# A deeper attention tail, norms two tiles ahead, padded denominators and warm-up matmuls in a four-layer kernel on one core

## Chip, cores, metric

The kernel runs on one core of one Trainium2 chip. The metric is the device time of one execution in microseconds (us); lower is better. A single-core program has one time per run; its runs are compared by their median, and a difference is called faster or slower only beyond 2%, with a 95% interval. All runs quoted are undisturbed ("fast").

Engine names as in the profile: PE is TensorE (matmuls), PEld its weight loads, DVE is VectorE, ACT is ScalarE, POOL is GpSimd, SP issues the DMAs.

## The reference

Four layers, A B A B, on x of 2048 tokens by 1024 features in bf16. A is linear attention with 32 heads of 32, B a gated linear unit with 3584 hidden features. The code is abridged here.

```python
def _A_ref(x, wqkv, wo):                       # x is layer-normed before the call
    q, k, v = split_heads(x @ wqkv)            # cut: reshape and transpose
    phi = lambda t: jnp.where(t > 0, t + 1, jnp.exp(t)) + 1e-6
    pq, pk = phi(q), phi(k)
    kv  = jnp.einsum("bhsd,bhse->bhde", pk, v)         # "KVA" below
    z   = jnp.einsum("bhsd->bhd", pk)
    num = jnp.einsum("bhqd,bhde->bhqe", pq, kv)        # "ND" below, with den
    den = jnp.einsum("bhqd,bhd->bhq", pq, z)[..., None] + 1e-6
    return merge_heads(num / den) @ wo                 # "OT", "WO" below

x = x + _A_ref(_layernorm(x), A_wqkv, A_wo)
x = x + _B_ref(_layernorm(x), B_w_gate, B_w_up, B_w_down)   # ((x Wg) * (x Wu)) Wd
# ... and both once more
```

## The kernel before

The program is recorded as a list of operations, each with the tiles that it reads and writes. From these the recorder derives dependencies, by *granules*: 256 bytes per partition in SBUF, one bank in PSUM. A list scheduler with estimated durations then fixes the order on each engine, and waits are emitted for the dependencies that the order doesn't cover. Note what it does for two operations on the same engine: TensorE is exempt from waiting on itself, the other engines are not.

```python
SB_GRAN = 256
...
        for d in sorted(op.deps, key=lambda o: -o.end):
            if d.eng == "pe" and e == "pe" and not d.dma_bytes:
                continue                       # no wait of PE on PE; DVE on DVE does wait
            if base.get(d.semkey, 0) >= d.sig:
                continue
            w.append((d.semkey, d.sig))
```

A layer A has three stages on TensorE. For each of 16 tiles of 128 tokens: the K and V projections (KVP, 32 matmuls of 512 columns) and the accumulation KVA (8 small matmuls). Then the Q projections (QP, 32 groups of 8). Then the *tail*: per tile ND (8 matmuls, numerator and denominator), a division on VectorE, OT (8 transposes), an eviction of OT from PSUM by ScalarE ("otev"), WO (16 matmuls of 512 columns), and the residual on VectorE. Layer norms run alongside, each ending in 8 transposes on TensorE (LT) and a copy on VectorE. In the first layer the norm of tile i is recorded just before the projections of tile i.

```python
    DEN = [view("DEN", r * SB_GRAN, H, F32) for r in range(2)]     # 32 floats, one granule
    RDEN = [view("RDEN", r * SB_GRAN, H, F32) for r in range(2)]
...
            if i + 1 < NT:                       # end of layer_A: the tail
                tail_pre(i + 1, par, kvb, 5)     # ND, division, OT, otev of the next tile
            tail_post(i, par, tb, [3, 4, 6])     # WO, residual, next norm of this tile
...
    def tail_pre(i, par, kvb, otbank):           # ND cut
            for k in range(nbk):                 # three PSUM banks
                dd = dn[:, 12 * k: 12 * k + 4 * n].rearrange(...)
                P.add("dve", ... eh.tensor_scalar(dd, src[:, :, 128:132], 1e-6, None, ALU.add), ...)
            P.add("dve", lambda eh, dn=dn, rd=rd: eh.reciprocal(rd, dn), ins=[dn], outs=[rd], ...)
            for (k, n, src) in srcs:             # o = numerator * reciprocal
                P.add("dve", ... eh.tensor_tensor(o4, n4, rb, ALU.mult), ...)
            P.add("pe", em_ot, ins=[ob, IDENT], outs=[pb[:, 0:NG * 128]], ...)
            P.add("act", ... eh.activation(otb, src, ACTF.Copy), ...)
```

## Time and profile before

| | before |
|---|---|
| median of 5 runs | 1714.61 us (1714.49 to 1714.73) |
| span of the profiled run | 1712.9 us |
| TensorE busy | 1687.5 us, 99% |
| late starts of TensorE, start and KV of layer one | 10.9 us |
| late starts of TensorE, both tails | 12.7 us |
| late starts elsewhere | under 0.5 us a stage |

"Late starts" needs a word. Matmuls are pipelined and their ends are modelled, so a TensorE that is "99% busy" may still lose time. But their starts come at a steady pace: 0.216 us for 512 columns, 0.056 to 0.059 us for 128 to 132. I took, from the trace, the gap between each matmul's start and the next one's, less the median gap for its source line, and summed by stage. That is the time that a change of order can win; the gated unit's stages have none.

From the page of the kernel before (busy table, then shares of the chain that ended last):

```profile
span 1712.9 us, 19994 instructions
...
PE 1687.5 (99%) x8704; PEld 799.2 (47%) x8704; DVE 749.0 (44%) x1227; ACT 356.3 (21%) x577; POOL 138.4 (8%) x261
...
PE 93%; ACT 3%; POOL 2%; issue 1%; DVE 0%; DMA 0%; POOLq 0%
```

The waits of TensorE in the kernel before (line that waited, who released it: us in total, times, longest):

```profile
PE ps L501 <- POOL arena L495: 8.8, 2, 8.6
PE ps L694 <- ACT arena L680: 7.9, 30, 0.7
PE ps L556 <- ACT arena L595: 2.9, 12, 0.2
```

L501 is LT, the first one behind the first norm. L694 is WO, waiting for the eviction of OT. L556 is KVA, waiting for the last V eviction.

The timeline of TensorE in the kernel before, at the start, in the KV stage of layer one and in the first tail (start us, duration us, engine, line, operation, count; in brackets the idle time before and what ended it):

```profile
8.65 1.04 PE L501 MATMUL ps<-arena 128*128 128x128 bf16 x8 [8.65 <-POOL arena L495]
10.47 6.38 PE L586 MATMUL ps<-arena 128*128 128x512 bf16 x16 [0.79 <-DVE arena L506]
...
62.15 0.64 PE L556 MATMUL ps<-arena 128*128 128x129 bf16 x8 [0.24 <-ACT arena L595]
...
70.46 0.63 PE L556 MATMUL ps<-arena 128*128 128x129 bf16 x8 [0.24 <-ACT arena L595]
...
223.13 3.63 PE L694 MATMUL ps<-arena 128*128 128x512 bf16 x16 [0.20 <-ACT arena L680]
226.59 0.61 PE L675 MATMUL ps<-arena 128*128 128x128 bf16 x8
227.04 0.61 PE L501 MATMUL ps<-arena 128*128 128x128 bf16 x8
227.49 0.63 PE L648 MATMUL ps<-arena 128*128 128x132 bf16 x8
228.32 1.04 PE L694 MATMUL ps<-arena 128*128 128x512 bf16 x4 [0.20 <-ACT arena L680]
```

Three readings. The first 16 KV matmuls take 6.38 us where 16 x 0.216 = 3.45 would do. A KV tile takes 70.46 - 62.15 = 8.31 us. A tail tile takes 228.32 - 223.13 = 5.19 us, of which the matmul starts fill 3.45 + 0.45 + 0.45 + 0.46 = 4.81; the rest stands before WO.

VectorE in the same tail tile of the kernel before (copy of LT, den, reciprocal, o, residual):

```profile
222.50 0.69 DVE L506 COPY arena<-ps 128x1024 bf16<-128x1024 bf16 x1 [0.19 <-PE ps L501]
223.11 0.56 DVE L661 TENSOR_SCALAR arena<-ps 128x12 f32<-128x12 f32 x3
223.71 0.35 DVE L663 RECIPROCAL arena<-arena 128x32 f32<-128x32 f32 x1
224.09 1.35 DVE L668 TENSOR_TENSOR arena<-ps,arena 128x384 bf16<-128x384 f32 x3
225.36 0.68 DVE L699 SCALAR_TENSOR_TENSOR arena<-ps,arena 128x512 f32<-128x512 f32 x1
```

The three den instructions of 0.16 to 0.17 us take 0.60 us until the reciprocal starts, so they don't overlap.

### The profile page before, as it was taken

To read this page: it belongs to the slowest core of one execution; us is meant where nothing else is said; L and a number is where in the kernel's file an instruction comes from. 1 tells how busy PE (TensorE), PEld (TensorE's weight loads), DVE (VectorE), ACT (ScalarE), POOL (GpSimd) and SP (SyncE) were. 2 spreads that over 40 slices of the span, in tenths; PEclk is the share of its full clock that TensorE was granted. 3 is DMA by queue.
4 is the path that set the end of the run, shared out by engine and by line. 5 is a ranking of instruction groups with operands and counts; after the bars stand their busy time and mean duration, and the time that the engine had idled before them with its cause. 6 is when DMAs were issued, how large, how long until landed. Compare 5 with 4: busy or idle time off the path is not lost.

```text
span 1712.9 us, 19994 instructions
## 1 busy us (share of the span) xinstructions
PE 1687.5 (99%) x8704; PEld 799.2 (47%) x8704; DVE 749.0 (44%) x1227; ACT 356.3 (21%) x577; POOL 138.4 (8%) x261
## 2 busy tenths in 40 slices
PE   7999999999999999999999999999999999999998
PEld 3444455444444444444454445544444444444444
DVE  7335775252424333333452367733343434242515
ACT  6323343101010111111343333421101010101010
POOL 5110043000000000000340001420000000000000
PEclk9999999999999999999999999999999999999999
DMA  7100102011010101020120001021010101010002
GB/s 251 44 1 1 50 1 75 28 47 49 25 50 25 49 25 49 25 74 25 50 75 1 1 1 50 1 74 50 25 50 25 50 25 50 25 49 25 1 24 99
DMA packets 55832, 70.49 MB, mean 41 GB/s; under 512 B 1472, under 2 KB 42432, under 8 KB 55744
## 3 DMA queue, kind: packets, MB, share of 16 engines
q1 hardware_dynamic: 55744, 69.21, 12.4%
q8 instruction: 68, 1.11, 0.3%
q14 instruction: 20, 0.16, 0.0%
HBM read 65.01 MB, written 4.19 MB: 40 GB/s over the span
## 4 chain that ended last, share of the span: by engine, by line
PE 93%; ACT 3%; POOL 2%; issue 1%; DVE 0%; DMA 0%; POOLq 0%
PE ps L730 45%; PE ps L753 21%; PE ps L586 12%; PE ps L694 7%; PE ps L624 6%; ACT arena L680 2%; POOL arena L495 1%; PE ps L556 1%; PE ps L675 1%; ACT arena L488 1%; POOL arena L492 1%; ACT arena L595 0%; PE ps L501 0%; POOL arena L490 0%; POOL arena L483 0%
## 5 line engine op out<-in xcount | busy, mean ns | idle before, releaser
L730 PE MATMUL ps<-arena 128*128 128x512 bf16 x3584 | 776.5, 379 | 0.0
L730 PEld LDWEIGHTS ps<-arena 128*128 128x128 bf16 x3584 | 350.4, 98 | 421.4
L739 DVE TENSOR_TENSOR arena<-ps,arena 128x512 bf16<-128x512 f32 x224 | 155.0, 692 | 601.5 <-PE ps L730 601.5
L753 PE MATMUL ps<-arena 128*128 128x512 bf16 x1792 | 390.9, 379 | 0.0
L737 ACT ACTIVATE arena<-ps 128x512 f32<-128x512 f32 x224 | 133.7, 597 | 964.0 <-PE ps L730 963.9
L759 DVE TENSOR_TENSOR arena<-ps,arena 128x1024 f32<-128x1024 f32 x192 | 235.2, 1225 | 102.8 <-PE ps L753 102.8
L753 PEld LDWEIGHTS ps<-arena 128*128 128x128 bf16 x1792 | 174.9, 98 | 208.8
L586 PE MATMUL ps<-arena 128*128 128x512 bf16 x1024 | 230.0, 382 | 0.8 <-DVE arena L506 0.8
L586 PEld LDWEIGHTS ps<-arena 128*128 128x128 bf16 x1024 | 98.6, 98 | 116.6 <-issue 3.6
L694 PE MATMUL ps<-arena 128*128 128x512 bf16 x512 | 116.1, 380 | 7.9 <-ACT arena L680 7.9
L512 DVE TENSOR_SCALAR arena<-arena 128x512 f32<-128x512 f32 x128 | 55.9, 436 | 145.7 <-ACT arena L511 145.7
L624 PE MATMUL ps<-arena 128*128 128x512 bf16 x512 | 111.5, 379 | 0.0
L511 ACT ACTIVATE arena<-ps 128x512 f32<-128x512 f32 x128 | 76.4, 597 | 165.3 <-PE ps L586 91.1
L514 DVE SCALAR_TENSOR_TENSOR arena<-ps,arena 128x512 bf16<-128x512 f32 x128 | 88.4, 691 | 3.9
L495 POOL TENSOR_SCALAR arena<-arena 128x1024 bf16<-128x1024 f32 x64 | 76.4, 1194 | 68.8 <-PE ps L501 63.7
L488 ACT ACTIVATE arena<-arena 128x1024 bf16<-128x1024 f32 x64 | 73.2, 1144 | 36.4 <-POOL arena L483 27.8
L694 PEld LDWEIGHTS ps<-arena 128*128 128x128 bf16 x512 | 47.6, 98 | 66.5 <-ACT arena L680 13.2
L624 PEld LDWEIGHTS ps<-arena 128*128 128x128 bf16 x512 | 49.9, 98 | 59.5
L506 DVE COPY arena<-ps 128x1024 bf16<-128x1024 bf16 x64 | 44.2, 690 | 41.3 <-PE ps L501 41.0
L699 DVE SCALAR_TENSOR_TENSOR arena<-ps,arena 128x512 f32<-128x512 f32 x64 | 44.0, 687 | 31.0 <-PE ps L694 31.0
L680 ACT ACTIVATE arena<-ps 128x1024 bf16<-128x1024 bf16 x32 | 32.8, 1024 | 92.9 <-PE ps L675 92.9
L483 POOL TENSOR_SCALAR arena<-arena 128x1 f32<-128x1 f32 x32 | 6.5, 202 | 560.2 <-DVE arena L763 550.2
(35 smaller groups left out, 434.2 us busy)
## 6 DMA issues: line engine op xcount, KB each, us to landing
arena<-in_B_w_gate_dram SPq DMA_DIRECT2D x14, 1024.0 KB, 5.4
arena<-in_B_w_up_dram SPq DMA_DIRECT2D x14, 1024.0 KB, 7.2
arena<-in_B_w_down_dram SPq DMA_DIRECT2D x14, 1024.0 KB, 5.5
arena<-in_A_x_dram SPq DMA_DIRECT2D x16, 256.0 KB, 3.3
arena<-in_A_wqkv_dram SPq DMA_DIRECT2D x8, 512.0 KB, 7.9
arena<-in_A_wqkv_dram SPq DMA_DIRECT2D x2, 2048.0 KB, 8.2
arena<-in_A_wo_dram SPq DMA_DIRECT2D x4, 1024.0 KB, 10.5
arena<-in_A_wqkv_dram SPq DMA_DIRECT2D x4, 1024.0 KB, 5.7
```

Of the source, the lines that this page charges most:

```text
L488: P.add("act", lambda eh: eh.activation(SQA, x, ACTF.Square, bias=st[:, 1:2], scale=1.0, accum_out=st[:, 2:3]), ins=[x, st[:, 1:2]], outs= ...
L495: P.add("pool", lambda eh: eh.tensor_scalar(lt, x, st[:, 1:2], st[:, 4:5], ALU.add, ALU.mult), ins=[x, st[:, 1:2], st[:, 4:5]], outs=[lt], ...
L511: P.add("act", lambda eh: eh.activation(et, pb_, ACTF.Exp), ins=[pb_], outs=[et], dur=act_t(fd), name="exp" + nm)
L514: P.add("dve", lambda eh: eh.scalar_tensor_tensor(dst, pb_, C1, et, ALU.add, ALU.max), ins=[pb_, et], outs=[(dst, dtag)], dur=dve_t(fd), n ...
L586: last = eh.matmul(pb_, LNT[:, dt_, i * 128:(i + 1) * 128], WKV[c][:, dt_, :], start=(dt_ == 0), stop=(dt_ == ND - 1))
L624: last = eh.matmul(pb_, WQ[:, dt_, g * 128:(g + 1) * 128], LNT[:, dt_, c * 512:(c + 1) * 512], start=(dt_ == 0), stop=(dt_ == ND - 1))
L694: last = eh.matmul(pb_, otb[:, g, :], WOW[cf][:, g, :], start=(g == 0), stop=(g == NG - 1))
L730: last = eh.matmul(pb_, W[:, dt_, jt * 128:(jt + 1) * 128], LNT[:, dt_, c * 512:(c + 1) * 512], start=(dt_ == 0), stop=(dt_ == ND - 1))
L737: P.add("act", lambda eh, gt=gt, pb_=pbs[0]: eh.activation(gt, pb_, ACTF.Copy), ins=[pbs[0]], outs=[gt], dur=act_t(512), name="gcp")
L739: P.add("dve", lambda eh, gt=gt, pb_=pbs[1], hd=hd: eh.tensor_tensor(hd, pb_, gt, ALU.mult), ins=[pbs[1], gt], outs=[(hd, "h%d" % jc)], du ...
L753: last = eh.matmul(pb_, HB[:, jt, i * 128:(i + 1) * 128], WD[:, jt, cf * FCW:(cf + 1) * FCW], start=(jt == 0), stop=(jt == 3))
L759: P.add("dve", lambda eh, i=i, acc=acc: eh.tensor_tensor(XRES[i], acc, XRES[i], ALU.add), ins=[acc, XRES[i]], outs=[XRES[i]], dur=dve_t(D) ...
```

## The change

The intent: keep TensorE from waiting. (1) 36 matmuls on a tile of ones while the first input is on its way, so that the clock is up when real work starts. (2) In the first layer, norms recorded two tiles ahead. (3) The tail split in two parts, with ND three tiles and OT two tiles ahead of WO. (4) den and rden slices 64 floats apart, so that each has a granule of its own, with one reciprocal per slice. Other buffers follow (three OT results; one set of statistics).

```diff
-HOIST = 2
+HOIST = 3
+NWARM = 36
...
-    alloc("O", 2 * D * 2); alloc("OTB", 2 * D * 2); ...
+    alloc("O", 2 * D * 2); alloc("OTB", 3 * D * 2); ...
-    DEN = [view("DEN", r * SB_GRAN, H, F32) for r in range(2)]
-    RDEN = [view("RDEN", r * SB_GRAN, H, F32) for r in range(2)]
+    DEN = [view("DEN", r * 3 * SB_GRAN, 192, F32) for r in range(2)]
+    RDEN = [view("RDEN", r * 3 * SB_GRAN, 192, F32) for r in range(2)]
...
+    def em_warm(eh):
+        for k in range(NWARM):
+            last = eh.matmul(bank(7, 256), onesb[:, 0:128], onesb[:, 0:256], start=True, stop=True)
+        return last
...
-                ln_chain(i, par, tb)
+                for ia in ([0, 1, 2] if i == 0 else [i + 2]):
+                    if ia < NT:
+                        first_ln(ia)
...
-                    tail_pre(0, par, kvb, tb)
+                    nd_part(0, par, kvb)
+                    ot_part(0, tb)
+                    if NT > 1:
+                        nd_part(1, par, kvb)
+                        ot_part(1, 5)
+                    if NT > 2:
+                        nd_part(2, par, kvb)
...
-            if i + 1 < NT:
-                tail_pre(i + 1, par, kvb, 5)
+            if i + 2 < NT:
+                ot_part(i + 2, 5)
+            if i + 3 < NT:
+                nd_part(i + 3, par, kvb)
             tail_post(i, par, tb, [3, 4, 6])
...
-            dd = dn[:, 12 * k: 12 * k + 4 * n]
+            dd = dn[:, 64 * k: 64 * k + 4 * n]
...
-        P.add("dve", lambda eh, dn=dn, rd=rd: eh.reciprocal(rd, dn), ins=[dn], outs=[rd], ...)
         for (k, n, src) in srcs:
+            P.add("dve", lambda eh, dk=dk, rk=rk: eh.reciprocal(rk, dk), ins=[dk], outs=[rk], ...)
```

More of the change, by code (lines that the diff above doesn't have):

```diff
@@ L387, in _build @@
     alloc("PK", NR * D * 2); alloc("VAUG", NR * NG * 132 * 2); alloc("ET", 4 * 512 * 4)
-    alloc("O", 2 * D * 2); alloc("OTB", 2 * D * 2); alloc("LNTOK", 2 * D * 2); lay["OUTS"] = lay["PK"]
+    alloc("O", 2 * D * 2); alloc("OTB", 3 * D * 2); alloc("LNTOK", 2 * D * 2); lay["OUTS"] = lay["PK"]
     alloc("KVZ", NG * 132 * 2); alloc("SQA", D * 2); lay["SQD"] = lay["O"]
-    alloc("DEN", 2 * SB_GRAN); alloc("RDEN", 2 * SB_GRAN); alloc("STAT", 2 * NT * SB_GRAN)
+    alloc("DEN", 2 * 3 * SB_GRAN); alloc("RDEN", 2 * 3 * SB_GRAN); alloc("STAT", NT * SB_GRAN)
     alloc("IDENT", 128 * 2); alloc("BMASK", 128 * 4); alloc("E4", 4 * 4); alloc("NEGH", 4); alloc("ONES", 128 * 4)
@@ L421, in _build @@
     XS = [view("O", r * D * 2, D, BF16) for r in range(4)]
-    OTB = [v3("OTB", r * D * 2, NG, 128, BF16) for r in range(2)]
+    OTB = [v3("OTB", r * D * 2, NG, 128, BF16) for r in range(3)]
     LNTOK = [view("LNTOK", r * D * 2, D, BF16) for r in range(2)]
@@ L427, in _build @@
     SQA = view("SQA", 0, D, BF16); SQD = view("SQD", 0, D, BF16)
-    DEN = [view("DEN", r * SB_GRAN, H, F32) for r in range(2)]
-    RDEN = [view("RDEN", r * SB_GRAN, H, F32) for r in range(2)]
-    STAT = [[view("STAT", (par * NT + i) * SB_GRAN, 8, F32) for i in range(NT)] for par in range(2)]
+    DEN = [view("DEN", r * 3 * SB_GRAN, 192, F32) for r in range(2)]
+    RDEN = [view("RDEN", r * 3 * SB_GRAN, 192, F32) for r in range(2)]
+    STAT = [[view("STAT", i * SB_GRAN, 8, F32) for i in range(NT)] for par in range(2)]
     IDENT = view("IDENT", 0, 128, BF16); BMASK = view("BMASK", 0, 128, F32)
@@ L470, in _build @@
           ins=[ONES], outs=[IDENT], dur=400, name="ident")
+    onesb = ONES.bitcast(BF16)
+    def em_warm(eh):
+        for k in range(NWARM):
+            last = eh.matmul(bank(7, 256), onesb[:, 0:128], onesb[:, 0:256], start=True, stop=True)
+        return last
+    if NWARM > 0:
+        P.add("pe", em_warm, ins=[ONES], outs=[bank(7, 256)], dur=NWARM * 150.0, name="warm")
     ctr = {"lntok": 0, "ring4": 0, "pair": 0, "pkv": 0, "et": 0, "o": 0, "otb": 0, "den": 0, "gu": 0, "dn": 0, "outs": 0, "wor": 0}
@@ L547, in late_loads, with first_ln @@
                 dma("sp", WOW[c][:], wo_src[:, :, c * FCW:(c + 1) * FCW], 128 * NG * FCW * 2, "ld_wo", tag="wo")
-        pend_kva = []
+        fl_state = {"rest": first_rest}
+        def first_ln(i):
+            if fl_state["rest"] is None:
+                late_loads()
+                fl_state["rest"] = []
+            for i2 in range(i, min(NT, i + 4)):
+                if i2 not in xslot:
+                    ldx(i2)
+                    fl_state["rest"].remove(i2)
+                    if not fl_state["rest"]:
+                        late_loads()
+            st = STAT[par][i]
+            P.add("dve", lambda eh, i=i, st=st, xs=xslot[i]: eh.tensor_scalar(XRES[i], xs, 1.0, None, ALU.mult, ALU.add, accum_out=st[:, 0:1]),
+                  ins=[xslot[i]], outs=[XRES[i], st[:, 0:1]], dur=dve_t(D), name="rowsum%d" % i)
+            if i == 0:
+                add_const1()
+            ln_chain(i, par, tb)
         def add_kva(i, r):
@@ L563, in layer_A @@
             if first:
-                if first_rest is None:
-                    late_loads()
-                    first_rest = []
-                for i2 in range(i, min(NT, i + 4)):
-                    if i2 not in xslot:
-                        ldx(i2)
-                        first_rest.remove(i2)
-                        if not first_rest:
-                            late_loads()
-                st = STAT[par][i]
-                P.add("dve", lambda eh, i=i, st=st, xs=xslot[i]: eh.tensor_scalar(XRES[i], xs, 1.0, None, ALU.mult, ALU.add, accum_out=st[:, 0:1]),
-                      ins=[xslot[i]], outs=[XRES[i], st[:, 0:1]], dur=dve_t(D), name="rowsum%d" % i)
-                if i == 0:
-                    add_const1()
-                ln_chain(i, par, tb)
+                for ia in ([0, 1, 2] if i == 0 else [i + 2]):
+                    if ia < NT:
+                        first_ln(ia)
             r = nxt("pkv", NR)
@@ L630, in layer_A @@
         if not hoisted:
-            tail_pre(0, par, kvb, 5)
+            nd_part(0, par, kvb)
+            ot_part(0, 5)
+            if NT > 1:
+                nd_part(1, par, kvb)
+                ot_part(1, 5)
+            if NT > 2:
+                nd_part(2, par, kvb)
         for i in range(NT):
-            if i + 1 < NT:
-                tail_pre(i + 1, par, kvb, 5)
+            if i + 2 < NT:
+                ot_part(i + 2, 5)
+            if i + 3 < NT:
+                nd_part(i + 3, par, kvb)
             tail_post(i, par, tb, [3, 4, 6])
@@ L638, in _build, with nd_part @@
     otbs = {}
-    def tail_pre(i, par, kvb, otbank):
+    obs = {}
+    def nd_part(i, par, kvb):
         nbk = (NG + 2) // 3
-        if True:
-            c, ii = i // 4, i % 4
-            def em_nd(eh, c=c, ii=ii):
-                for g in range(NG):
-                    lh = PQT[c][:, g, ii * 128:(ii + 1) * 128]
-                    last = eh.matmul(bank(kvb[g // 3], 132, (g % 3) * 132), lh, KVZ[:, g, 0:132], start=True, stop=True)
-                return last
-            P.add("pe", em_nd, ins=[(PQT[c][:, :, ii * 128:(ii + 1) * 128], "pqt"), KVZ[:]], outs=[bank(kvb[k]) for k in range(nbk)],
-                  dur=NG * 58.0, name="ND%d" % i)
-            r = nxt("den", 2)
-            dn, rd = DEN[r], RDEN[r]
-            ob = OB[nxt("o", 2)]
-            srcs = []
-            for k in range(nbk):
-                n = min(3, NG - 3 * k)
-                src = ps[:, kvb[k] * 512: kvb[k] * 512 + n * 132].rearrange("p (a b) -> p a b", a=n)
-                srcs.append((k, n, src))
-                dd = dn[:, 12 * k: 12 * k + 4 * n].rearrange("p (a b) -> p a b", a=n)
-                P.add("dve", lambda eh, dd=dd, src=src: eh.tensor_scalar(dd, src[:, :, 128:132], 1e-6, None, ALU.add),
-                      ins=[src[:, :, 128:132]], outs=[dn[:, 12 * k: 12 * k + 4 * n]], dur=120, name="den%d" % i)
-            P.add("dve", lambda eh, dn=dn, rd=rd: eh.reciprocal(rd, dn), ins=[dn], outs=[rd], dur=65 + 8 * H / 0.96, name="rden%d" % i)
-            for (k, n, src) in srcs:
-                o4 = ob[:, 384 * k: 384 * k + 128 * n].rearrange("p (a h e) -> p a h e", a=n, h=4)
-                n4 = src[:, :, 0:128].rearrange("p a (h e) -> p a h e", h=4)
-                rb = rd[:, 12 * k: 12 * k + 4 * n].rearrange("p (a h) -> p a h", a=n).unsqueeze(3).to_broadcast([128, n, 4, 32])
-                P.add("dve", lambda eh, o4=o4, n4=n4, rb=rb: eh.tensor_tensor(o4, n4, rb, ALU.mult),
-                      ins=[src[:, :, 0:128], rd[:, 12 * k: 12 * k + 4 * n]], outs=[ob[:, 384 * k: 384 * k + 128 * n]],
-                      dur=dve_t(128 * n), name="o%d" % i)
-            pb = bankb(otbank)
-            def em_ot(eh, ob=ob, pb=pb):
-                for g in range(NG):
-                    last = eh.transpose(pb[:, g * 128:(g + 1) * 128], ob[:, g * 128:(g + 1) * 128], IDENT)
-                return last
-            P.add("pe", em_ot, ins=[ob, IDENT], outs=[pb[:, 0:NG * 128]], dur=NG * 56.0, name="OT%d" % i)
-            otb = OTB[nxt("otb", 2)]
-            src = pb[:, 0:NG * 128].rearrange("p (a b) -> p a b", a=NG)
-            P.add("act", lambda eh, otb=otb, src=src: eh.activation(otb, src, ACTF.Copy), ins=[src], outs=[otb[:]],
-                  dur=act_t(NG * 128), name="otev%d" % i)
-            otbs[i] = otb
@@ new lines, in nd_part, with em_nd @@
+        c, ii = i // 4, i % 4
+        def em_nd(eh, c=c, ii=ii):
+            for g in range(NG):
+                lh = PQT[c][:, g, ii * 128:(ii + 1) * 128]
+                last = eh.matmul(bank(kvb[g // 3], 132, (g % 3) * 132), lh, KVZ[:, g, 0:132], start=True, stop=True)
+            return last
+        P.add("pe", em_nd, ins=[(PQT[c][:, :, ii * 128:(ii + 1) * 128], "pqt"), KVZ[:]], outs=[bank(kvb[k]) for k in range(nbk)],
+              dur=NG * 58.0, name="ND%d" % i)
+        r = nxt("den", 2)
@@ new lines, in nd_part @@
+        dn, rd = DEN[r], RDEN[r]
+        ob = OB[nxt("o", 2)]
+        obs[i] = ob
+        srcs = []
+        for k in range(nbk):
+            n = min(3, NG - 3 * k)
+            src = ps[:, kvb[k] * 512: kvb[k] * 512 + n * 132].rearrange("p (a b) -> p a b", a=n)
+            srcs.append((k, n, src))
+            dd = dn[:, 64 * k: 64 * k + 4 * n].rearrange("p (a b) -> p a b", a=n)
+            P.add("dve", lambda eh, dd=dd, src=src: eh.tensor_scalar(dd, src[:, :, 128:132], 1e-6, None, ALU.add),
+                  ins=[src[:, :, 128:132]], outs=[dn[:, 64 * k: 64 * k + 4 * n]], dur=120, name="den%d" % i)
@@ new lines, in nd_part @@
+        for (k, n, src) in srcs:
+            dk = dn[:, 64 * k: 64 * k + 4 * n]
+            rk = rd[:, 64 * k: 64 * k + 4 * n]
+            P.add("dve", lambda eh, dk=dk, rk=rk: eh.reciprocal(rk, dk), ins=[dk], outs=[rk], dur=65 + 8 * 4 * n / 0.96, name="rden%d" % i)
+            o4 = ob[:, 384 * k: 384 * k + 128 * n].rearrange("p (a h e) -> p a h e", a=n, h=4)
+            n4 = src[:, :, 0:128].rearrange("p a (h e) -> p a h e", h=4)
+            rb = rk.rearrange("p (a h) -> p a h", a=n).unsqueeze(3).to_broadcast([128, n, 4, 32])
+            P.add("dve", lambda eh, o4=o4, n4=n4, rb=rb: eh.tensor_tensor(o4, n4, rb, ALU.mult),
+                  ins=[src[:, :, 0:128], rk], outs=[ob[:, 384 * k: 384 * k + 128 * n]],
+                  dur=dve_t(128 * n), name="o%d" % i)
@@ new lines, in ot_part, with em_ot @@
+    def ot_part(i, otbank):
+        ob = obs[i]
+        pb = bankb(otbank)
+        def em_ot(eh, ob=ob, pb=pb):
+            for g in range(NG):
+                last = eh.transpose(pb[:, g * 128:(g + 1) * 128], ob[:, g * 128:(g + 1) * 128], IDENT)
+            return last
+        P.add("pe", em_ot, ins=[ob, IDENT], outs=[pb[:, 0:NG * 128]], dur=NG * 56.0, name="OT%d" % i)
+        otb = OTB[nxt("otb", 3)]
+        src = pb[:, 0:NG * 128].rearrange("p (a b) -> p a b", a=NG)
+        P.add("act", lambda eh, otb=otb, src=src: eh.activation(otb, src, ACTF.Copy), ins=[src], outs=[otb[:]],
+              dur=act_t(NG * 128), name="otev%d" % i)
+        otbs[i] = otb
```

## The prediction

> **What bounds the kernel now.** The busy table puts TensorE at 99% of a 1712.9 us span; in the timeline a 512-column matmul starts every 0.216 us, a 128-column one every 0.056 to 0.059. Summing starts later than that pace, I find only some 23 us to win; the GLU stages have none.
> - Start: the first transpose begins at 8.65 us, behind input load, rowsum, square and norm (chain of waits). The first 16 KV matmuls take 6.38 us instead of 3.45, the first eight transposes about 0.9 instead of 0.45: half clock. The Trainium skill, "TensorE: Matmul & The Clock Gate", Part 1, says that an idle array runs at half clock until about 3.4 us of sustained activity[...].
> - First layer's KV stage: a tile takes 8.31 us, in the second layer 7.37. The difference is a transpose group (0.45) and about 0.5 lost before the KV accumulation, which waits for the last V eviction on ScalarE.
> - The two attention tails: a tile takes 5.19 us against 4.81 of matmul starts (WO 3.45, three small groups 0.45 each). The loss stands before WO, waiting for the 1.02 us ScalarE eviction of OT (waits list: 7.9 us over 30 waits; 12.7 with exposed weight loads).
>
> **What the change does.**
> 1. Warm-up: 36 matmuls of 256 columns from about 1.1 us. At half clock (0.21 us each) they take at most 7.7 us and end near or before 8.65, delaying nothing. The idle gaps after them, under 2 us, should not bring half clock back. Gain 2.9 us in KV and 0.4 in the first transpose. By landing times in the trace the third weight block arrives at 14.6 us and will now be wanted at 13.9: 0.75 back.
> 2. Layer norms run two tiles ahead. In the built order a KV accumulation stands 2.2 us after the V projection instead of 0.45. The wait goes: 0.5 us in some 11 tiles plus 1.2 earlier, about 6.5 us.
> 3. Tail: OT moves a tile ahead of WO, so its eviction hides behind a whole WO. But VectorE gets two more instructions a tile (three small reciprocals, about 0.2 us each, for one of 0.35) and becomes critical: in its built order the last piece of o, which the next OT needs, stands behind the first WO residual. The loop from durations in the trace: transpose copy 0.61, den 0.60, reciprocals 0.63, o 1.35, residual 0.73, OT 0.45, transpose to copy 0.65: about 5.05 us a tile. TensorE waits 0.25 us before OT instead of 0.38 before WO. Gain 0.12 x 12 x 2, about 3 us.
> 4. Tail heads get worse: the last Q projection uses OT's PSUM bank and now stands behind an OT eviction (about 0.8 us), and ND waits for o. I add 1.2 us per tail.
>
> Sum: start 2.5, KV 6.5, tails 3 less 2.5: about 10 us, all critical, since TensorE is.
>
> **Prediction.** 1704 us, 8 in 10 between 1697 and 1709. Faster by over 2%: 0.01; within 2%: 0.98; slower by over 2%: 0.01. Even the whole 23 us is 1.4%.
>
> **Right or wrong in the profile.** First KV group of 16 in about 3.5 us, starting near 10.0; a KV tile of layer one at 7.8 us; in the tails a period of 5.0 to 5.1 us, with the wait on ScalarE replaced by one on VectorE before OT; VectorE over 90% busy there; GLU stages unchanged.
>
> **What would make it wrong.** VectorE closing the loop faster (tail at 4.82: 6 us better), or slower than 5.19; half clock returning before the first KV group (3 us worse); input loads starving the faster start.

## The result

| | before | after |
|---|---|---|
| median | 1714.56 us (13 runs, 1713.3 to 1715.2) | 1695.66 us (7 runs, 1695.3 to 1697.5) |
| ratio of fast runs | | 0.9893, 95% interval 0.9883 to 0.9903 |
| span of the profiled run | 1712.9 us | 1694.0 us |
| late starts, start and KV of layer one | 10.9 us | 2.05 us |
| late starts, both tails | 12.7 us | 3.0 us |

A ratio is the mean time of one kernel's fast runs over that of the other's of the same rounds, so it is not quite the ratio of the medians. The late starts of the new kernel are counted from the first transpose on, so the warm-up is not in them.

The change wins 18.9 us. I had 1704, with 1697 to 1709 as range: the time lies below it. The late starts say where the miss is. Start and KV won 8.9 us where I had 9.0; the tails won 9.7 us where I had a net 0.5. Within a tail, the kernel before lost 0.85 and 0.81 us in late starts at the head and 0.36 us in each of 13 later tiles; the changed kernel loses the same 0.85 and 0.81 at the head and nothing after it.

From the page of the changed kernel:

```profile
span 1694.0 us, 20158 instructions
...
PE 1683.4 (99%) x8740; PEld 803.2 (47%) x8740; DVE 743.1 (44%) x1291; ACT 357.7 (21%) x577; POOL 138.8 (8%) x261
...
PE 97%; POOL 1%; DMA 1%; ACT 0%; SPq 0%; issue 0%; DVE 0%; POOLq 0%
```

VectorE has 64 more instructions than before and is busy 5.9 us less. A reader who expects more work from more instructions should stop here. The busy time of an engine counts overlapping instructions once; these have begun to overlap. Added up singly, the durations of den, reciprocals and o rose from 75.8 to 82.9 us, while the time that they cover fell from 70.5 to 65.6.

The waits of TensorE in the changed kernel:

```profile
PE ps L729 <- ACT arena L715: 1.4, 2, 0.7
PE ps L645 <- ACT arena L715: 1.3, 2, 0.6
...
PE ps L601 <- DMA arena<-in_A_wqkv_dram: 0.7, 1, 0.7
```

L729 (WO) and L645 (QP) wait for OT's eviction twice each, at the head of each tail and never again. No wait of TensorE on VectorE before OT (L710) is in the list, and that wait was the heart of my third step.

The timeline of TensorE in the changed kernel: start, KV stage, head of the first tail, steady tail:

```profile
8.58 0.62 PE L511 MATMUL ps<-arena 128*128 128x128 bf16 x8 [0.45 <-POOL arena L505]
10.33 3.63 PE L601 MATMUL ps<-arena 128*128 128x512 bf16 x16 [1.13 <-DVE arena L516]
...
15.11 3.63 PE L601 MATMUL ps<-arena 128*128 128x512 bf16 x16 [0.71 <-DMA arena<-in_A_wqkv_dram]
...
60.29 0.62 PE L583 MATMUL ps<-arena 128*128 128x129 bf16 x8
...
68.11 0.62 PE L583 MATMUL ps<-arena 128*128 128x129 bf16 x8
...
191.59 3.63 PE L729 MATMUL ps<-arena 128*128 128x512 bf16 x16 [0.69 <-ACT arena L715]
...
196.78 1.90 PE L645 MATMUL ps<-arena 128*128 128x512 bf16 x8 [0.65 <-ACT arena L715]
...
226.95 0.61 PE L710 MATMUL ps<-arena 128*128 128x128 bf16 x8
...
231.76 0.61 PE L710 MATMUL ps<-arena 128*128 128x128 bf16 x8
```

The first KV group now takes 3.63 us. A KV tile takes 68.11 - 60.29 = 7.82 us, without idle time before KVA. A tail tile takes 231.76 - 226.95 = 4.81 us, the bare pace of its matmuls.

VectorE in that tail tile of the changed kernel:

```profile
228.04 0.69 DVE L516 COPY arena<-ps 128x1024 bf16<-128x1024 bf16 x1 [0.19 <-PE ps L511]
228.65 0.31 DVE L691 TENSOR_SCALAR arena<-ps 128x12 f32<-128x12 f32 x3
228.88 0.31 DVE L696 RECIPROCAL arena<-arena 128x12 f32<-128x12 f32 x2
229.13 1.02 DVE L700 TENSOR_TENSOR arena<-ps,arena 128x384 bf16<-128x384 f32 x2
230.07 0.19 DVE L696 RECIPROCAL arena<-arena 128x8 f32<-128x8 f32 x1
230.24 0.69 DVE L734 SCALAR_TENSOR_TENSOR arena<-ps,arena 128x512 f32<-128x512 f32 x1
...
230.85 0.42 DVE L700 TENSOR_TENSOR arena<-ps,arena 128x256 bf16<-128x256 f32 x1
```

The same three den instructions now take 0.23 us until the reciprocal starts, and the two reciprocals 0.25 together. Each single den lasts as long as before (0.16 us); the next one starts 0.077 us after its start instead of 0.20. The order is as I had read it, with the last piece of o behind the residual. But the chain from the copy to the end of that piece is 231.27 - 228.04 = 3.23 us, where I had counted 3.92. OT starts 0.49 us after it.

What differs in the built programs: before, 64 of the 96 den instructions carry a wait of VectorE on VectorE. They write the same granule as the den before them and are therefore taken to conflict with it. After, none of the 96 does. The padding, which I had passed over as bookkeeping, removes these waits. It doesn't remove all waits of VectorE on itself: 60 of the 96 reciprocals and all 96 o still carry one. But their starts lie closer together than they last (mostly 0.13 us for two reciprocals of 0.19, 0.475 for two o of 0.55), so these waits are met before they hold anything up.

### The profile page after: what moved, and what is told of

Same layout as the page of the kernel before. It is cut to its first block, busy times and chain, and to the rows that moved or that the text cites. A ratio compares the mean times of both kernels' runs of the same rounds, so it can differ in the third digit from the quotient of the medians.

```text
span 1694.0 us, 20158 instructions
## 1 busy us (share of the span) xinstructions
PE 1683.4 (99%) x8740; PEld 803.2 (47%) x8740; DVE 743.1 (44%) x1291; ACT 357.7 (21%) x577; POOL 138.8 (8%) x261
## 4 chain that ended last, share of the span: by engine, by line
PE 97%; POOL 1%; DMA 1%; ACT 0%; SPq 0%; issue 0%; DVE 0%; POOLq 0%
PE ps L765 46%; PE ps L788 22%; PE ps L601 13%; PE ps L645 7%; PE ps L729 7%; PE ps L511 1%; PE ps L583 1%; PE ps L710 1%; PE ps L677 1%; DMA arena<-in_A_wqkv_dram 1%; POOL arena L505 0%; SPq L451 0%; ACT arena L715 0%; POOL arena L502 0%; POOL arena L500 0%
## 5 line engine op out<-in xcount | busy, mean ns | idle before, releaser
L729 PE MATMUL ps<-arena 128*128 128x512 bf16 x512 | 116.0, 379 | 1.4 <-ACT arena L715 1.4
L645 PE MATMUL ps<-arena 128*128 128x512 bf16 x512 | 111.8, 379 | 1.3 <-ACT arena L715 1.3
L645 PEld LDWEIGHTS ps<-arena 128*128 128x128 bf16 x512 | 49.8, 98 | 60.7 <-ACT arena L715 1.6
L729 PEld LDWEIGHTS ps<-arena 128*128 128x128 bf16 x512 | 48.6, 98 | 54.4 <-ACT arena L715 1.7
L610 ACT ACTIVATE arena<-ps 128x512 bf16<-128x512 f32 x64 | 38.1, 596 | 64.6 <-PE ps L601 64.1
```

Source lines behind the costliest of these rows:

```text
L645: last = eh.matmul(pb_, WQ[:, dt_, g * 128:(g + 1) * 128], LNT[:, dt_, c * 512:(c + 1) * 512], start=(dt_ == 0), stop=(dt_ == ND - 1))
L729: last = eh.matmul(pb_, otb[:, g, :], WOW[cf][:, g, :], start=(g == 0), stop=(g == NG - 1))
```

## The experiments

Times are medians; "before" ran in the same rounds at 1714.1 to 1714.7. The changed kernel ran in other rounds than the experiments. Late-start figures and periods come from the traces. All outputs are right.

The questions. **Theory:** the tail is fast because the padding removes VectorE's waits on itself, which lets the deeper order run at TensorE's pace. **Rivals:** I mis-counted the loop and the layout plays no part; or the packed addresses themselves are slow; or the padding alone did it and the deeper order is idle. And for the rest: what warm-up and earlier norms are worth.

### e1_no_warm: the change without the warm-up

```diff
-NWARM = 36
+NWARM = 0
```

> The changed kernel (1695.7 us) without its 36 warm-up matmuls. Theory: they are worth the half-clock start, 2.9 us in the first 16 KV matmuls and 0.4 in the first transposes, less 0.7 for the third weight block, whose wait vanishes when the start is slow: 1698.2 us (1697.3 to 1699.2), the first 16 KV matmuls in about 6.4 us, no wait on the weight DMA. Rival: the earlier clock only moves the wait to the weight DMA, so it is worth under 1 us: below 1696.7.

Measured 1698.05 us (1697.0 to 1698.3), so the warm-up is worth 2.4 us. The weight DMA is gone from the list of waits, as the theory had it. In the profiled run the first KV group took 5.51 us rather than 6.4, and started later, at 11.13; the clock's rise falls differently in each run.

### e2_no_ahead: norms one tile at a time again

```diff
-                for ia in ([0, 1, 2] if i == 0 else [i + 2]):
-                    if ia < NT:
-                        first_ln(ia)
+                first_ln(i)
```

> The changed kernel with the layer norm of tile i back in front of tile i instead of two tiles ahead; all else kept. Theory: the KV accumulation again stands one transpose group after the V projection and waits about 0.5 us a tile: KV tile of layer one at 8.3 us instead of 7.8, total 1701.5 us (1700 to 1703). Rival: the warm-up had taken most of the gain of this stage, then the loss is 2 us or less: below 1698.

Measured 1702.89 us (1702.5 to 1703.2). KVA waits for the V eviction in 12 tiles again, and late starts in the KV stage past 50 us return to 5.27 us, the figure of the kernel before. The earlier norms are worth 7.2 us; I had 6.5.

### e5_old_tail: old tail order, padding kept

```diff
-HOIST = 3
+HOIST = 2
...
-            if i + 2 < NT:
-                ot_part(i + 2, 5)
-            if i + 3 < NT:
-                nd_part(i + 3, par, kvb)
+            if i + 1 < NT:
+                nd_part(i + 1, par, kvb)
+                ot_part(i + 1, 5)
```

> The changed kernel with the old tail order (ND and OT of tile i+1 directly before WO of tile i, hoist 2), but with the padded den and rden and the split reciprocals kept. Theory: the padding alone gains nothing, since the old order waits for the OT eviction on ScalarE: tail tile 5.19 us as before, 1704.5 us (1703.5 to 1706). Rival: the padding and not the deeper order made the tail fast: tail tile 4.9 or less, below 1699.

Measured 1705.41 us (1704.5 to 1707.2); a tail tile takes 5.19 us again, with TensorE waiting on ScalarE before WO (7.7 us over 29 waits). The deeper order is worth 9.75 us on top of the padding. The three parts, each taken out alone, are worth 2.4 + 7.2 + 9.75 = 19.4 us against 18.9 measured together: they add up within the spread.

### e10_pad_only: padding and split reciprocal alone on the kernel before

This is e5_old_tail with the edits of e1_no_warm and e2_no_ahead as well; the changed buffer counts (three OT results, one set of statistics) stay too.

> The kernel before with one part of the change alone: den and rden padded to a granule per slice and the reciprocal split in three. Theory: VectorE gains time, but the old tail waits on the OT eviction on ScalarE, so a tail tile stays at 5.19 us: 1714.5 us within 1. Rival: the padding makes the tail faster on its own: below 1711.

Measured 1714.12 us against 1714.14, ratio 1.0001 (0.9986 to 1.0016). The tail tile stays at 5.19 us. The padding alone is worth nothing: the old order waits for ScalarE, and a faster VectorE only idles longer.

### e3_packed: the change with den and rden packed again

```diff
-            dd = dn[:, 64 * k: 64 * k + 4 * n]      (and every other such slice of dn and rd)
+            dd = dn[:, 12 * k: 12 * k + 4 * n]
```

> The changed kernel with the den and rden slices packed again (12 columns apart, one tracked granule) in place of 64 columns apart. Theory: packing brings back the waits of VectorE on its own earlier writes (den starts 0.2 us apart, not 0.08), the VectorE loop grows from about 4.4 us to about 5.0, and the tail tile from 4.82 to about 5.0 with TensorE waiting on VectorE: plus 4 us, 1699.7 (1697.5 to 1702). Rival (I just over-counted the small reciprocals or the loop; the layout plays no part): period 4.82, 1695.7 within 0.7.

Measured 1714.89 us (1713.7 to 1716.4), ratio to before 1.0003. The direction is the theory's, the size is not: packing costs 19.2 us, as much as the whole change wins. The waits of TensorE show why:

```profile
PE ps L729 <- ACT arena L715: 11.1, 24, 0.6
```

WO waits for the OT eviction again, and more than in the old tail: late starts of 0.81 and 0.36 us alternate from tile to tile where the kernel before had 0.36. With the warm-up and the earlier norms still in, the run is 9.5 us above e5_old_tail. In the old order the padding is worth nothing (e10_pad_only), so the deeper order without the padding is worse than the old order. With one granule the second reciprocal must also wait until the o before it has read the first one, and so on; the recorder's scheduler sees a longer chain, finds OT not ready when TensorE is free, and places it just before its own WO. The depth that the source asks for is not in the built order. So this run changed two things, the waits and the order. The next three take out both, or add waits in unchanged order.

### e4_packed_fine: packed addresses, finer tracking

```diff
     tag = "p" if is_ps else "s"
+    if not is_ps and FINE[0] <= off * ds < FINE[1]:     # DEN and RDEN only
+        gran, tag = 16, "f"
```

on top of e3_packed.

> The packed den and rden of e3_packed, but their dependencies are tracked in 16-byte pieces, so that slices that don't overlap are not taken as conflicting. The built order of every engine equals the changed kernel's. If the wait and order that the shared 256-byte granule causes are the cost (theory): 1695.7 us within 1, tail tile 4.82, den starts 0.08 us apart. If the packed addresses themselves are slow (rival): den starts stay 0.2 us apart, tail tile above 4.9 and the total above 1700.

Measured 1695.57 us (1695.0 to 1697.9), den starts 0.077 us apart. The order of every engine equals that of the changed kernel. So the addresses don't matter; the false dependency does. Padding was one way to remove it, finer tracking is another.

### e7_own_waits and e8_own_waits_den: the changed kernel with waits added

```diff
             for k2, v2 in wm.items():
                 eh.wait_ge(semh(k2), v2)
+            if op.name.rstrip("0123456789") in OWN:      # e7: den, rden, o; e8: den
+                eh.wait_ge(sems[eng_name], op.sig - 1)   # the instruction before, same engine
```

Order and layout stay the same in both; only the waits differ.

> The changed kernel in unchanged order and layout, with one thing added: each den, reciprocal and o of the tail waits on VectorE's own instruction before it (a wait that is always met in the end, so the result stays right). Theory: a wait on one's own engine ends the overlap of instructions; the chain copy, den, reciprocals, o, residual, o grows by about 1.0 us against a slack of 0.44 us, so the tail tile goes to about 5.4 us and the total to 1709 us (1705 to 1713), TensorE waiting on VectorE before OT. Rival (own waits are free, only the other order made e3_packed slow): 4.82 and 1695.7 within 1.

Measured 1719.19 us (1718.8 to 1719.5), slower than the kernel before. From the timelines of VectorE and then TensorE in e7_own_waits:

```profile
224.10 0.69 DVE L519 COPY arena<-ps 128x1024 bf16<-128x1024 bf16 x1 [0.56 <-PE ps L514]
224.90 0.58 DVE L694 TENSOR_SCALAR arena<-ps 128x12 f32<-128x12 f32 x3
...
228.37 0.42 DVE L703 TENSOR_TENSOR arena<-ps,arena 128x256 bf16<-128x256 f32 x1
```

```profile
223.00 0.62 PE L713 MATMUL ps<-arena 128*128 128x128 bf16 x8 [1.03 <-DVE arena L703]
...
228.85 0.62 PE L713 MATMUL ps<-arena 128*128 128x128 bf16 x8 [0.87 <-DVE arena L703]
```

The chain from copy to the end of o is 228.79 - 224.10 = 4.69 us, 1.46 more than in the changed kernel (I had expected 1.0; the measured 1719.19 us also lies above the 1705 to 1713 that I had expected). A tail tile takes 5.85 us, and TensorE waits on VectorE before OT, 14.4 us over 24 waits: exactly the wait that I had predicted for the changed kernel. The loop exists; the changed kernel is only on the right side of it.

> As e7_own_waits, with the added wait on the three den instructions alone. Theory: the chain grows by about 0.36 us, less than the 0.44 us of slack that the trace of the changed kernel shows before OT, so nothing is lost: tail tile 4.82, 1695.7 us within 1, den starts 0.2 us apart. Rival (VectorE is as full as predicted, no slack): tail tile 5.05 or more, above 1699.

Measured 1696.30 us (1695.4 to 1696.7), the same as the changed kernel. From VectorE's timeline in e8_own_waits_den:

```profile
228.52 0.69 DVE L519 COPY arena<-ps 128x1024 bf16<-128x1024 bf16 x1 [0.19 <-PE ps L514]
229.32 0.58 DVE L694 TENSOR_SCALAR arena<-ps 128x12 f32<-128x12 f32 x3
...
231.67 0.42 DVE L703 TENSOR_TENSOR arena<-ps,arena 128x256 bf16<-128x256 f32 x1
232.44 0.69 DVE L737 SCALAR_TENSOR_TENSOR arena<-ps,arena 128x512 f32<-128x512 f32 x1 [0.34 <-PE ps L732]
```

The chain has grown to 232.09 - 228.52 = 3.57 us, by 0.34. Add 0.06 from the end of o to OT (228.79 to 228.85 in e7_own_waits) and 1.09 from OT to the next copy (226.95 to 228.04 in the changed kernel), and the loop is 4.72 us, below the 4.81 of TensorE: nothing is lost. The same sum gives 3.23 + 1.15 = 4.38 for the changed kernel and 4.69 + 1.15 = 5.84 for e7_own_waits, against 5.85 measured. So the den waits alone would not have made the tail slow; 0.43 us of room was there. It takes waits on the reciprocals and o as well, as in e7_own_waits, to slow it.

### e6_ot1_bank7: a better head of the tail

```diff
-                        ot_part(1, 5)
+                        ot_part(1, tb)
                     if NT > 2:
                         nd_part(2, par, kvb)
```

(the first of two such places; tb is bank 7)

> The changed kernel with the second tile's OT in PSUM bank 7 instead of bank 5, so that the last Q projection no longer stands behind that OT's eviction and fills the wait for the first one. Theory: both head waits of each tail (0.85 and 0.81 us) go, with perhaps 0.3 us of waiting for o in their place: 1692.9 us (1692 to 1694). Rival (the head waits move to another wait of the same length): 1695.7 within 0.7.

Measured 1692.89 us (1692.0 to 1694.5). In the changed kernel the last Q projection writes the PSUM bank that the second OT uses, so it stands behind that OT's eviction (the 0.65 us wait at 196.78 above), while TensorE has nothing to fill the first wait (0.69 at 191.59). With another bank, it moves into that gap:

```profile
191.18 1.89 PE L645 MATMUL ps<-arena 128*128 128x512 bf16 x8
192.91 1.89 PE L729 MATMUL ps<-arena 128*128 128x512 bf16 x8
```

Both head waits are gone in both tails, without a new one.

### e9_x2_later: a wait that went without gain

```diff
-                if xq and c < 3:
+                if xq and c in (0, 2):
+                    ldx(xq.pop(0))
+                if xq and c == 2:
                     ldx(xq.pop(0))
```

on top of e6_ot1_bank7.

> The kernel of e6_ot1_bank7 (1692.9 us) with the load of the third input tile moved behind the third weight block, so that this block lands 0.7 us earlier. Theory: the wait of TensorE on the weight DMA (0.75 us) goes and the third norm is still ready in time: 1692.2 us (1691.3 to 1693.2). Rival: TensorE then waits for the third input tile's norm instead, 1 us or more: 1692.9 or above, with a wait of a transpose on the normalising engine of over 0.5 us at about 20 us.

Measured 1692.71 us (1691.9 to 1693.5). The wait on the weight DMA is gone from the list, but the time moved by less than the spread, so no gain is shown. Its profile shows something else. The clock records of that run, as windows (us; busy time and instructions by engine; then granted clock, DMA share, GB/s):

```profile
4.40:7.70 3.30, 2.38 (x22) 1.89 (x20) 0.44 (x2) 1.24 (x2) 1.22 (x4) 1.00 1.04 355
7.80:11.10 3.30, 1.07 (x11) 0.67 (x12) 1.83 (x3) 0.80 (x1) 1.00 (x2) 1.00 1.10 349
11.20:14.50 3.30, 3.30 (x10) 1.12 (x8) 0.07 (x1) 0.94 (x3) 1.94 (x3) 0.50 1.08 364
```

The full clock came at 4.36 us, the warm-up matmuls ended early, and at 11.19 us the clock fell back to half for 3.41 us: its first KV group took 5.31 us. My prediction had named that risk and thought it unlikely, because no single gap exceeds 2 us. Two gaps, 1.89 us and 1.36 us, lie in and around one stretch of 3.4 us, 7.77 to 11.19, in which TensorE was busy 1.16 us (1.07 in the 3.30 us shown). In the profiled run of the changed kernel, the stretch of 3.4 us after the rise at 7.13 us had 1.84 us of work, and the clock stayed up. The moment of the rise varies between profiled runs: with the same 36 warm-up matmuls it came 3.25 us after the first of them here and 6.0 us in the changed kernel, and so the warm-up ended at 6.78 us here and at 8.13 there.

### e11_fill: work in the gap

```diff
             ln_chain(i, par, tb)
+            if i == 0:
+                add_fill()      # 8 more matmuls on ones after the first LT, into bank 6
```

on top of e6_ot1_bank7.

> The kernel of e6_ot1_bank7 with 8 more idle matmuls of 256 columns between the first transposes and the first KV group, where TensorE waits 1.1 to 1.5 us for VectorE. Theory: the runs 1.8 us above the rest (1694.5 of e6, 1697.4 of the changed kernel) are those in which the clock fell back to half in that gap, as the profile of e9 shows at 11.2 us; with the gap filled no run is slow: all runs within 1691.5 to 1693.5, first KV group in 3.6 us. Rival (other causes of the spread, input landing times say): spread stays about 2.5 us.

Measured 1692.05 us, and all four runs lie between 1691.83 and 1692.25. The spread of 0.4 us stands against 2.5 us for e6_ot1_bank7. The upper group of times is gone, as the theory had it, but that is not shown: in the changed kernel 3 of 8 runs were in that group and in e6_ot1_bank7 1 of 4, so four low runs can be chance. The record leans the theory's way: the high run of e6_ot1_bank7 has a mean granted clock of 0.998, the others 0.999 to 1.0. This is the lowest median, with a ratio to before of 0.9872 (0.9855 to 0.9888), an interval that overlaps those of e6_ot1_bank7 and e9_x2_later. The median lies 3.6 us below that of the changed kernel, measured in other rounds.

### e12_warm16: a short warm-up

```diff
-NWARM = 36
+NWARM = 16
```

> The changed kernel with 16 warm-up matmuls instead of 36: at half clock they end at about 4.5 us, 4 us ahead of the first transposes. Theory: the half clock is there when the first KV group starts, so nothing is gained over e1_no_warm: 1698 us (1697 to 1698.7), first 16 KV matmuls in 5.3 us or more. Rival (any 3.4 us of activity since the start is enough): 1695.7 within 0.7.

Measured 1697.14 us (1696.6 to 1698.1). Windows of its profile:

```profile
4.80:8.10 3.30, 0.00 (x0) 0.00 (x0) 0.00 (x0) 1.24 (x2) 1.73 (x4) 1.00 0.99 333
8.20:14.90 6.70, 5.56 (x19) 2.40 (x20) 3.32 (x6) 2.14 (x4) 2.60 (x6) 0.50 1.09 365
```

The warm-up did raise the clock, at 4.72 us, just when it had ended. The full clock was granted for 3.41 us in which TensorE did nothing, and was gone before the first transpose at 8.55. The first KV group took 5.88 us. The time lies within the expected range and above the rival's; against e1_no_warm (1698.05) the difference of 0.9 us is within the spread of both. A warm-up is worth what it leaves at the moment of use.

## Why the prediction was wrong

- **Start (step 1): right, in part by luck.** Predicted net 2.5 us, measured 2.4 (e1_no_warm). The weight wait came as foreseen (0.71 us against 0.75). The Trainium skill, "TensorE: Matmul & The Clock Gate", Part 1, on the half clock of an idle array is borne out: the warm-up matmuls start 0.213 us apart at first and about 0.11 us apart after the rise. Its 3.4 us of sustained activity is not the time to reckon with: from the first warm-up matmul to the rise the profiled runs show 3.25 to 6.0 us, and in the kernel before the rise came at 16.06 us, 5.6 us after the first KV matmul. The luck is in when that rise falls: e9_x2_later, with the same warm-up, lost the clock again. The page's section "Why this matters for your kernels" advises against idle gaps beyond about 3 us; I built on that, and e9_x2_later shows that the clock can fall after shorter gaps close together.
- **Norms ahead (step 2): right.** Predicted 6.5 us, measured 7.2 (e2_no_ahead). A KV tile takes 7.82 us; I had said 7.8.
- **Tail (step 3): wrong, and this is the miss.** The mechanism of the first half was right: OT's eviction hides behind a WO. The failed step is "VectorE ... becomes critical: ... The loop from durations in the trace: ... about 5.05 us a tile". The loop is real (e7_own_waits shows it at work), but it measures 4.38 us. Term by term, as start-to-start times of the changed kernel: copy 0.61 (I had 0.61), den 0.23 (0.60), reciprocals 0.25 + 0.17 = 0.42 (0.63), o 1.36 (1.35), residual 0.62 (0.73), and from the end of o to the next copy 1.15 (1.10). Three terms were too big, by 0.37, 0.21 and 0.11 us. I had taken the den spacing from a program in which two of three den wait for the one before, and assumed it for a program in which none does. The reciprocals I had summed as durations of about 0.2 us each, but they overlap too; why the residual was 0.11 too big is not on record. By this sum no term decides it alone: TensorE needs 4.81 us a tile, so there were 0.43 us of room, and e8_own_waits_den, with the den waits back, is still fast. It took the errors together to put the loop above TensorE's pace. So the gain was 0.38 us in 13 of 16 tiles and not 0.12. My list of what would make it wrong had named this outcome ("tail at 4.82: 6 us better"). VectorE, expected over 90% busy there, was busy 39.3 of 48.1 us, 82%.
- **Why it was avoidable.** The durations were in the trace beside the starts: three instructions of 0.16 us that start 0.20 us apart don't overlap, and one asks why. The built program lists the waits; 64 den instructions had one before and none after. I compared the order and not the waits, and passed over the padding in the diff. It is half of what makes the deeper order work: alone it gains nothing (e10_pad_only), and without it the deeper order loses 9.5 us against the old order (e3_packed against e5_old_tail).
- **A page I could have tested.** The Trainium skill, "VectorE: DVE Perf Modes", section "The DRAIN you can't avoid", says that the next instruction doesn't start until the pipe is empty, and that leaving out semaphores gains nothing; its section "Rules for kernel authors" repeats it. The trace disagrees for small instructions (0.077 us against 0.20 us) and for two o in a row (0.475 us apart in the changed kernel, 0.66 in e7_own_waits), and the measurement decides. The same section also says that an instruction that is not held starts earlier, and refers to the section "Two Vector instructions with no wait between them"; this is what the trace shows.
- **Tail heads (step 4): wrong in the sum.** The Q projection behind the OT eviction came as foreseen: 0.81 us a tail in late starts. But in the kernel before the second WO lost the same 0.81 us there, and the first WO 0.85 in both kernels; and ND doesn't wait for o. So the heads cost the same before and after, and the 1.2 us a tail that I added, 2.4 in all, was not there.
- **Left open.** e3_packed was not split further into the part due to waits and the part due to order. How much work in a stretch of 3.4 us keeps the clock up was not tested. The clock records narrow it: after 1.16 us (e9_x2_later) and 1.13 us (the end of e6_ot1_bank7) it fell, after 1.46 us (the end of e2_no_ahead) and 1.84 us (changed kernel) it stayed. Whether the sum of the work is what counts is not shown.

## What to carry to other kernels

Where a recorder derives dependencies from coarse granules, small tiles that share a granule wait for each other on their own engine; before timing a chain of small instructions, look at the distance between starts against the durations, and at the waits in the built program. Durations read from a trace belong to the waits of that program: carry them to a changed program only where its waits are the same. And a warm-up has to hold until the work begins: fill the gap in front of the work, not only the time before it.

## What the Trainium skill lacked or had wrong

- "VectorE: DVE Perf Modes", sections "The DRAIN you can't avoid" and "Rules for kernel authors": that chaining without semaphores gains nothing. For 12-column instructions of 0.16 us a wait on the engine's own previous instruction costs 0.13 us each (starts 0.077 us apart without, 0.20 with; changed kernel and e8_own_waits_den). Over den, reciprocals and o it lengthened the chain by 1.46 us a tile (e7_own_waits).
- "TensorE: Matmul & The Clock Gate", section "Why this matters for your kernels": no gaps beyond about 3 us. The length of single gaps isn't enough: in e9_x2_later the clock fell to half after a stretch of 3.4 us with gaps of only 1.89 and 1.36 us in and around it, in which TensorE was busy 1.16 us. With 1.84 us of work in such a stretch it stayed up (changed kernel).
- The same page's advice on warming up gives a length and does not say that it must reach to the work: with 16 matmuls the full clock was granted for 3.41 us of idleness and gone before use (e12_warm16). With eight matmuls in the gap, four runs spread over 0.4 us instead of 2.5 (e11_fill; too few to show the cause).
